# Splitting two loads of output weights into eight shares instead of sixteen, in a decode-attention kernel

## The chip, the cores and the metric

One core of a Trainium2 chip. The time is the device time of one execution, in microseconds (us); most executions of this program agree within 0.4 us. All runs used here were fast (within 1.5% of the fastest run of the same kernel). Traces come from profiled executions, which took as long as the others.

## The reference, cut to what matters

The kernel computes two decode-attention blocks, A and B, for a batch of 4 with one query token each, and puts their outputs side by side:

```python
# shortened: block B; A lets four query heads share each of its key-value heads
q = (x @ wq).reshape(B, Sq, H, Dh).transpose(0, 2, 1, 3)
scores = einsum("bhqd,bhkd->bhqk", q, k_cache) * Dh ** -0.5
o = einsum("bhqk,bhkd->bhqd", softmax(scores), v_cache)
out = o.transpose(0, 2, 1, 3).reshape(B, Sq, H * Dh) @ wo
```

B has 32 heads of 128 and reads all 8192 cached positions; A has 8 key-value heads and reads the last 2048. B's keys and values alone are 537 MB, so this is a kernel of loads.

## The kernel before

The parts that the change touches. B's work goes by pairs of heads (`hp`, 16 of them) and by batch entry; a pair's two heads of one entry are one load of keys and one of values, 4 MB each, 128 partitions of 32 KB. The output weights of a pair are 256 KB, 128 partitions of 2 KB, in a single-buffered tile `wos`:

```python
def dma_wos(hp):
    src = B_wo[2 * hp * P:2 * (hp + 1) * P, :].rearrange("(p r) n -> p (r n)", r=2)
    sch.add_dma("sp", lambda e: e.dma_start(wos[:, :, :].rearrange("p r n -> p (r n)"), src), "d_wos",
                waits=[("fin", NCA + 4 * hp - 1)] if hp else [], key=("wos", hp))
# ... (cut)
for kind, c in loads:
    if kind == "k" and c >= NCA and (c == NCA or (c - NCA) % 4 == 3 and c > NCA + 3):
        dma_wos((c - NCA) // 4)
    dma_kv(kind, c)
```

All large loads are issued from SyncE's queue in this order. The kernel counts a load as landed when its semaphore has gained 16. The trace of before shows the sixteen: each load has sixteen landing marks, and the queue has 2804 packets of 4 bytes (9 ns each), 16 for each of its 175 loads and 4 for a store of 4 rows.

## Time and profile before

| | before |
|---|---|
| time, median (lowest to highest) of 6 runs | 1374.13 us (1373.97 to 1374.33) |
| bytes read | 587.2 MB, 428 GB/s over the span |
| SyncE's queue, share of 16 DMA engines' time | 99.8% |
| TensorE busy | 86% |

The lines and their reading are in the prediction below.

### The profile page before, as it was taken

What the parts mean: (1) busy time and instruction counts of PE and PEld (TensorE: products, weight loads), DVE (VectorE), ACT (ScalarE), POOL (GpSimd) and SP (SyncE); (2) the same over time, 40 slices, a digit from 0 to 9 for tenths busy, and PEclk for the clock granted to TensorE, in tenths of its full rate; (3) what the DMA queues carried; (4) which work ended last, traced back from release to release, by engine and by line L of the source; (5) the groups of instructions that cost most, each with busy time, mean ns of one, the idle gap of its engine ahead of it and who ended that gap; (6) DMA issues with size and microseconds to landing.
All of it is one profiled execution on the core that took longest, in us unless ns stands there. A gap on an engine that the chain in (4) does not pass through costs nothing.

```text
span 1372.6 us, 59967 instructions
## 1 busy us (share of the span) xinstructions
PE 1176.5 (86%) x27065; PEld 1132.9 (83%) x27067; DVE 656.6 (48%) x1434; ACT 434.7 (32%) x650; POOL 7.3 (1%) x28
## 2 busy tenths in 40 slices
PE   4888898889888888988888888888898888888888
PEld 4777898888888888888888878888898888888888
DVE  1775454445444444454445444444454444444544
ACT  1553232333223322332233323322333233323322
POOL 2000000000000000000000000000000000000000
PEclk9998999999999999999999999999999999999999
DMA  9999999999999999999999999999999999999998
GB/s 400 423 424 432 429 433 428 433 432 432 432 431 433 429 434 428 434 430 434 430 434 430 430 433 432 432 431 433 429 433 431 434 429 434 430 432 432 432 427 352
DMA packets 25261, 587.53 MB, mean 428 GB/s; under 512 B 2820, under 2 KB 2840, under 8 KB 6296
## 3 DMA queue, kind: packets, MB, share of 16 engines
q1 hardware_dynamic: 25208, 587.22, 99.8%
q8 instruction: 16, 0.26, 0.1%
q14 instruction: 5, 0.04, 0.0%
q10 hardware_dynamic: 32, 0.01, 0.0%
HBM read 587.21 MB, written 0.01 MB: 428 GB/s over the span
## 4 chain that ended last, share of the span: by engine, by line
DMA 65%; PE 33%; issue 1%; DVE 1%; ACT 0%; SPq 0%; DVEq 0%
DMA kv<-in_B_k_cache_dram 57%; PE tr L408 21%; PE sc L410 9%; DMA kv<-in_A_k_cache_dram 5%; DMA kv<-in_B_v_cache_dram 3%; PE po L410 2%; PE fin L410 1%; PE ms L410 0%; ACT kt L476 0%; DVE sA L527 0%; SPq L365 0%; ACT pba L597 0%; PE ms L408 0%; DVE zA L683 0%; DVE rm L536 0%
## 5 line engine op out<-in xcount | busy, mean ns | idle before, releaser
L408 PE MATMUL tr<-identb,kv 128*128 128x128 bf16 x8704 | 697.9, 230 | 148.8 <-DMA kv<-in_B_k_cache_dram 141.5
L478 DVE COPY kt<-tr 128x1024 bf16<-128x1024 bf16 x736 | 502.6, 690 | 457.1 <-PE tr L408 452.7
L408 PEld LDWEIGHTS tr<-identb,kv 128*128 128x128 bf16 x8704 | 552.9, 104 | 165.2 <-DMA kv<-in_B_k_cache_dram 81.7
L476 ACT ACTIVATE kt<-tr 128x1024 bf16<-128x1024 bf16 x352 | 359.3, 1023 | 666.8 <-PE tr L408 666.7
L410 PE MATMUL sc<-qb,kt 128*128 128x64 bf16 x8704 | 446.2, 196 | 14.3 <-ACT kt L476 12.8
L410 PEld LDWEIGHTS sc<-qb,kt 128*128 128x128 bf16 x8704 | 366.4, 100 | 26.0 <-ACT kt L476 20.2
L410 PE MATMUL po<-pbb,kv 128*128 128x64 bf16 x8320 | 284.4, 192 | 4.5 <-issue 3.9
L410 PEld LDWEIGHTS po<-pbb,kv 128*128 128x128 bf16 x8320 | 263.2, 97 | 7.1 <-issue 4.1
L577 ACT ACTIVATE pbb<-sc,negb 64x128 bf16<-64x128 f32 x128 | 51.6, 403 | 254.3 <-DVE negb L564 253.5
L541 DVE TENSOR_REDUCE rm<-sc 64x1 f32<-64x128 f32 x128 | 37.0, 289 | 56.6 <-PE sc L410 55.7
L553 DVE TENSOR_REDUCE gm<-ms 1x2 f32<-1x128 f32 (+1 forms) x72 | 20.1, 279 | 48.4 <-PE ms L408 48.4
L564 DVE COPY negb<-ms 128x1 f32<-128x1 f32 (+1 forms) x72 | 11.4, 158 | 47.0 <-PE ms L410 46.8
L410 PE MATMUL ms<-identf,gx 1*128 1x1 f32 (+1 forms) x144 | 27.2, 256 | 0.8 <-DVE zA L683 0.8
L666 DVE TENSOR_TENSOR oz<-po,rz 128x8 bf16<-128x8 f32 x33 | 5.5, 166 | 40.7 <-PE po L410 40.7
L410 PEld LDWEIGHTS ms<-identf,gx 1*128 1x128 f32 (+1 forms) x144 | 21.1, 182 | 4.6 <-DVE zA L683 0.9
L577 ACT ACTIVATION_READ_ACCUMULATOR pbb<-sc,negb 64x1 f32 x128 | 23.7, 185 | 0.0
L410 PE MATMUL po<-pba,kv 128*128 128x64 bf16 x512 | 20.5, 199 | 3.5 <-issue 2.1
L410 PEld LDWEIGHTS po<-pba,kv 128*128 128x128 bf16 x512 | 17.9, 102 | 5.7 <-ACT pba L597 4.2
L408 PE MATMUL ms<-identf,rm 128*1 128x128 f32 (+1 forms) x72 | 19.5, 271 | 2.4 <-DVE rm L536 2.3
L557 DVE TENSOR_SCALAR gx<-gm 1x128 f32<-1x128 f32 (+1 forms) x72 | 16.0, 222 | 2.5
L683 DVE CAST zB<-ms 64x8 bf16<-64x8 f32 x64 | 10.5, 164 | 9.2 <-PE ms L410 8.7
L410 PE MATMUL ms<-xT,kv 128*128 128x4 bf16 x256 | 7.1, 166 | 8.8 <-DMA kv<-in_A_wq_dram 5.0
(61 smaller groups left out, 173.9 us busy)
## 6 DMA issues: line engine op xcount, KB each, us to landing
kv<-in_B_k_cache_dram SPq DMA_DIRECT2D x63, 4096.0 KB, 26.5
kv<-in_B_v_cache_dram SPq DMA_DIRECT2D x63, 4096.0 KB, 30.9
kv<-in_A_k_cache_dram SPq DMA_DIRECT2D x8, 2048.0 KB, 14.8
kv<-in_A_v_cache_dram SPq DMA_DIRECT2D x8, 2048.0 KB, 16.2
kv<-in_A_wq_dram SPq DMA_DIRECT2D x1, 4096.0 KB, 12.5
kv<-in_B_wq_dram SPq DMA_DIRECT2D x1, 4096.0 KB, 27.1
wor<-in_A_wo_dram SPq DMA_DIRECT2D x8, 512.0 KB, 9.8
wos<-in_B_wo_dram SPq DMA_DIRECT2D x16, 256.0 KB, 20.3
```

Source lines behind the costliest of these rows:

```text
L408: sch.add("pe", lambda e: e.transpose(o, l, r), waits, key)
L410: sch.add("pe", lambda e: e.matmul(o, l, r, start=start, stop=stop), waits, key)
L476: sch.add("act", lambda e: e.activation(dst, src, ACTF.Copy), waits=waits, key=("ev", s))
L478: sch.add("dve", lambda e: e.tensor_copy(dst, src), waits=waits, key=("ev", s))
L541: sch.add("dve", lambda e, src=src, pp=pp: e.tensor_reduce(out=rm[pp, m, 0:1], in_=src, axis=AX.X, op=ALU.max), waits=[("S", ch["s_last"]) ...
L553: sch.add("dve", lambda e: e.tensor_reduce(out=gm[0:C, m, 0:U], in_=src, axis=AX.X, op=ALU.max), waits=[("trm", c)], key=("gmax", c))
L557: sch.add("dve", lambda e: e.tensor_scalar(out=dst, in0=gv, scalar1=-scale, scalar2=None, op0=ALU.mult), waits=[("gmax", c)], key=("gx", c))
L564: sch.add("dve", lambda e: e.tensor_copy(negb[:, m, 0:C], ms[:, col:col + C]), waits=[("bc", c)], key=("negb", c))
L577: sch.add("act", lambda e, src=src, pp=pp, n=n, u=u: e.activation(probs_of(c)[pp, :, u], src, ACTF.Exp, bias=negb[pp, m, 0:1], scale=scale ...
L666: sch.add("dve", lambda e: e.tensor_tensor(out=o, in0=i0, in1=i1, op=ALU.mult), waits=waits, key=("oT", c))
L683: sch.add("dve", lambda e, src=src, pp=pp: e.tensor_copy(z[pp, :].rearrange("p (r b) -> p r b", r=k), src), waits=[("sm", c)] + free if h ...
```

## The change

The intent: move some bytes away from half of the DMA engines. If a load's source has an outer dimension of 8, its rows should be dealt out in eight shares to eight engines, and the other eight would be left free.

```diff
             src = B_wo[2 * hp * P:2 * (hp + 1) * P, :].rearrange("(p r) n -> p (r n)", r=2)
-            sch.add_dma("sp", lambda e: e.dma_start(wos[:, :, :].rearrange("p r n -> p (r n)"), src), "d_wos",
+            dst = wos[:, :, :].rearrange("p r n -> p (r n)")
+            if hp in (1, 2):
+                (s, _), (x, n) = src.ap
+                src = bass.AP(src.tensor, src.offset, [[16 * s, 8], [s, 16], [x, n]])
+            sch.add_dma("sp", lambda e: e.dma_start(dst, src), "d_wos",
                         waits=[("fin", NCA + 4 * hp - 1)] if hp else [], key=("wos", hp))
```

An access pattern is a list of [step, count]. `s` is the step from one row to the next, so `[16 * s, 8], [s, 16]` names the same 128 rows in the same order as `[s, 128]`.

## The prediction

> **What bounds the kernel now.** I read the page's slices first (part 2), then the queues (part 3), then the chain of waits, then the times at which each load landed.
>
> ```profile
> PE   4888898889888888988888888888898888888888
> PEclk9998999999999999999999999999999999999999
> DMA  9999999999999999999999999999999999999998
> GB/s 400 423 424 432 429 433 428 433 432 432 432 431 433 429 434 428 434 430 434 430 434 430 430 433 432 432 431 433 429 433 431 434 429 434 430 432 432 432 427 352
> ...
> q1 hardware_dynamic: 25208, 587.22, 99.8%
> q8 instruction: 16, 0.26, 0.1%
> q14 instruction: 5, 0.04, 0.0%
> ...
> DMA 65%; PE 33%; issue 1%; DVE 1%; ACT 0%; SPq 0%; DVEq 0%
> ```
>
> The DMA row is at 9 in 39 of 40 slices and the rate stays at 427 to 434 GB/s through the middle. One queue, SyncE's, fills the time of all 16 DMA engines (99.8%). TensorE is busy too, but the chain of waits is mostly DMA, and its last part is a load:
>
> ```profile
> 1329.13 0.43 SPq L365
> 1329.56 0.35 issue
> 1329.92 39.14 DMA kv<-in_B_v_cache_dram
> 1369.06 0.05 issue
> 1369.11 0.42 PE po L410 x8
> ```
>
> The last piece of values is issued at 1329.92 us and lands at 1369.06; 3.5 us of small work follow to the end at 1372.6. So the end is the moment at which the last byte lands, plus a fixed tail. Loads are never issued too late to keep the engines fed: in the table of issues a 4 MB load of keys lands 26.5 us after its issue and one of values 30.9 us, while the engines need 4194 KB / 432 GB/s = 9.7 us for one, so two to three loads are always queued ahead.
>
> ```profile
> kv<-in_B_k_cache_dram SPq DMA_DIRECT2D x63, 4096.0 KB, 26.5
> kv<-in_B_v_cache_dram SPq DMA_DIRECT2D x63, 4096.0 KB, 30.9
> ...
> wos<-in_B_wo_dram SPq DMA_DIRECT2D x16, 256.0 KB, 20.3
> ```
>
> A load counts as landed when the **last** of its 16 engines is done, so I looked at the engines one by one. The trace has no engine number, but every packet starts 4 ns before the end of the one ahead of it on its engine, and every engine gets the same sequence of sizes, so the packets can be sorted into 16 chains. At the last large load of keys (landing at about 1343 to 1347 us) the chains stand behind the earliest by (us, worked out):
>
> ```
> eight chains without a q8 packet in the body: 0.00 0.06 0.20 0.34 0.34 0.56 1.40 2.13
> eight chains with q8 packets:                 1.96 3.15 3.25 3.28 3.32 3.38 3.41 3.81
> ```
>
> The trace's sixteen landing marks of each load say the same: first to last 0.8 us at 12 us, 2.3 us at 43 us, 3.8 us at 144 us, and 3.7 us ever after. The steps fall where a q8 packet (16 KB of instructions) goes: 15 of them between 19.7 and 168.2 us, each setting its chain back by about 1.5 us, going round the same eight chains in the same order. Seven of these chains are hit twice, one once. After 168 us [...]no more come until 1368 us. The two stragglers among the other eight carry q14 packets (8 KB; at 55 and 151 us on one, at 83 and 1333 us on the other). So eight engines end late because of work that isn't the kernel's data, and the change is about shifting data to the others.
>
> [...]the 4-row loads of x and the 4-row store at 128 us left exactly 4 data packets each. The four chains of that store are 0.00, 0.20, 1.40 and 2.13 of the list above (matched by the phase of their packets)[...]. [...]q8 shows 16 packets of 16384 bytes. [...]
>
> **The change, part by part.** It removes nothing: the same 256 KB go to the same rows of the weight tile, for pairs 1 and 2 (issued at 220.1 and 298.5 us). No instruction of TensorE, VectorE or ScalarE moves, no wait is added. What changes is the split: [...]with 16 rows of 2 KB on each of engines 0 to 7 and nothing on 8 to 15.
> - One share of eight rows costs an engine 8 packets x 84 ns (median of the 2 KB packets) = 0.67 us less overlaps of 4 ns each, plus a 9 ns mark: 0.65 us. The landing marks give 0.66 us (values at 316.08, weights at 316.74, first engine). I use 0.66.
> - Each changed load puts engines 0 to 7 back by 0.66 us and brings 8 to 15 forward by 0.66 us. Two: 1.32 us each way, and it stays, as spreads stay once made.
> - If the first line is engines 0 to 7 and the second 8 to 15, the latest of the second becomes 3.81 - 1.32 = 2.49, the latest of the first 2.13 + 1.32 = 3.45. The last landing moves from 3.81 to 3.45: **0.36 us earlier**. One split load alone would give max(3.15, 2.79), 0.66 us; the second overshoots because of the one chain with two q14 packets.
> - SyncE's issue of a weight load takes 0.33 us[...]. It lies beside 20 us of queued loads and costs nothing.
>
> Sum: 1374.1 - 0.36 = 1373.7 us. Perfect balance would put all chains at their mean of 1.91, a gain of 1.9 us or 0.14%, so this lever can't reach 2% in either direction.
>
> **The rivals.**
> - *The late eight aren't 8 to 15.* [...]If the instruction queue used, say, engines 4 to 11, some of the late chains would get 1.32 us more: 3.81 + 1.32 = 5.13, the end 1.3 us later, 1375.4 us. Against it: [...]the author chose exactly eight shares. I give it 1 in 8.
> - [...]Then the late eight lose by contention what they gain by skipping, nothing improves, and the time is 1374.1 to 1374.4. [...]I give it 1 in 6.
> - *The q14 stragglers come at other places* in unprofiled executions. Without them the first line's latest would be about 0.6 + 1.3 = 1.9, the second's 2.49 rules, and the full 1.32 us is gained: 1372.8 us. 1 in 10.
> - *The transfer is hidden anyway*, TensorE being the bound. Then nothing moves: 1374.1 us. Against it, TensorE's transposes sat idle 141.5 us waiting for keys of B.
>
> **Range and chances.** Three runs before lie within 0.36 us of each other, as much as the gain that I expect, so the sign is hardly to be seen in a median. The rivals span 1372.8 to 1375.4. I take 1373.7, with 1372.8 to 1375.0 for 8 in 10, which leaves out most of the wrong-half case. Two per cent are 27 us; no case comes near, so 0.99 for within 2%.
>
> **What would show it.** In the changed kernel's profile: (1) the count of 2 KB packets stays (2 x 128), but in each of the two loads 8 landing marks come from the engines and not 16, so the table of issues may lose its landing time for the weights; (2) landings of keys after 240 us come some 0.66 us earlier than before, and after 317 us about 0.36 us earlier, no further gain; (3) the spread of a load's sixteen marks, 3.8 us at 232 us before, falls to about 3.2 after the first and is about 3.4 after the second, with the order turned over: the former first line last; (4) 32 KB packets near 240 and 318 us not stretched beyond 1.22 us, or the port rival holds; (5) a spread grown to 5 us would be the wrong half. The prediction is wrong if the end moves by over 1.3 us, for which an engine would have to starve or the copy be split otherwise than in eight.

The forecast's sum is 1374.1 - 0.36 = 1373.7 us. Its premise: each of the two loads goes out in eight shares to eight engines; take that as the author's assumption. All that the trace shows towards it is that the copies of 4 rows left 4 data packets and 4 landing marks each. The trace numbers no engines: read "0 to 7" as the eight that such a load was expected to use, "8 to 15" as the others. That "0 to 7" are the first line of the list was assumed too. The second rival, called ports from here on, had an engine write, with its neighbouring rows, partitions that others were writing at that time, and both slow down.

## The result, and the profile after

| | before | after |
|---|---|---|
| time, median of 6 runs | 1374.13 us | 1374.14 us |
| lowest to highest | 1373.97 to 1374.33 | 1374.03 to 1374.33 |

The ratio of after to before is 1.0 (95% interval 0.9987 to 1.0013): the same. Ratios here are the mean time of one kernel's fast runs over that of the other's fast runs of the same rounds, so not quite the ratio of the medians.

From the page of the kernel after, the slices and the queues (packets, MB, share of 16 engines' time), and the issues of the weights (KB, median us to landing):

```profile
DMA  9999999999999999999999999999999999999998
...
DMA packets 25261, 587.53 MB, mean 428 GB/s; under 512 B 2820, under 2 KB 2840, under 8 KB 6296
...
q1 hardware_dynamic: 25208, 587.22, 99.8%
...
wos<-in_B_wo_dram SPq DMA_DIRECT2D x16, 256.0 KB, 20.6
```

The queue has the same 25208 packets as before. That is the line that gives it away. The 4-byte packets among them are the landing marks, one for each engine that takes part in a load: 16 for each of the 175 loads, as before. A load on eight engines has eight marks fewer, so two of them should have left 25192, the count that two real splits left later (next section). And the landing time of the weights is still there, 20.6 us; on the page of those two real splits it is missing.

The chain of waits at the end (start, duration, what) ends as before's does. The last piece was issued 1.0 us earlier and took 0.9 us longer; its landing is before's to within 0.2 us:

```profile
1328.88 40.05 DMA kv<-in_B_v_cache_dram
1368.94 0.05 issue
1368.98 0.42 PE po L414 x8
```

The last byte lands at 1368.94 us; before it was 1369.06. For the engines one by one I use the trace's sixteen landing marks of a load (us behind the first), here those of the keys that follow the first changed load, worked out from the trace. Below, a chain is the sequence of packets of one DMA engine:

```
before  248.06 + 0.0 0.1 0.3 0.3 0.4 0.4 0.9 2.0 2.2 3.1 3.3 3.3 3.3 3.5 3.5 3.8
after   248.54 + 0.0 0.0 0.0 0.2 0.3 0.4 1.5 1.5 1.6 2.7 2.8 2.9 2.9 3.0 3.1 3.2
```

The spread after looks smaller, as the prediction had hoped. But the last load of keys *ahead* of the changed one has the same 3.25 us, first to last (before's has 3.85). The difference was there before the change could act; it is one execution against another.

Then I compared the two built programs, instruction by instruction. They differ in source lines and tracebacks and in nothing else. The source of the two loads, as built, in elements:

```
before                   [[1024, 128], [1, 1024]]
after                    [[1024, 128], [1, 1024]]
reordered (next section) [[1024, 8], [8192, 16], [1, 1024]]
```

The eight by sixteen, which walks on evenly, was folded into 128 again in the build; the reordered one, which doesn't, was left as it is.

### The profile page after: what moved, and what is told of

Its sections match the earlier page's. It is cut to its first block, busy times and chain, and to the rows that moved or that the text cites. A ratio compares the mean times of both kernels' runs of the same rounds, so it can differ in the third digit from the quotient of the medians.

```text
span 1372.4 us, 59967 instructions
## 1 busy us (share of the span) xinstructions
PE 1177.7 (86%) x27065; PEld 1135.4 (83%) x27067; DVE 656.5 (48%) x1434; ACT 435.3 (32%) x650; POOL 7.4 (1%) x28
## 3 DMA queue, kind: packets, MB, share of 16 engines
q1 hardware_dynamic: 25208, 587.22, 99.8%
## 4 chain that ended last, share of the span: by engine, by line
DMA 60%; PE 37%; issue 1%; DVE 1%; ACT 1%; SPq 0%; DVEq 0%
DMA kv<-in_B_k_cache_dram 55%; PE tr L412 23%; PE sc L414 9%; DMA kv<-in_B_v_cache_dram 3%; PE po L414 2%; DMA kv<-in_B_wq_dram 2%; PE fin L414 1%; PE ms L414 1%; DVE sA L531 0%; ACT kt L480 0%; DVE rm L540 0%; PE ms L412 0%; SPq L369 0%; DVE sA L529 0%; ACT pba L601 0%
## 6 DMA issues: line engine op xcount, KB each, us to landing
wos<-in_B_wo_dram SPq DMA_DIRECT2D x16, 256.0 KB, 20.6
```

## The experiments

Theory **folded**: the change never reached the chip, so nothing can be learnt from its time about shares of eight. Rival **balanced**: the shares were eight, and gains and losses cancelled. Beyond that, two models of what real shares of eight would do: **engines** (the prediction's: bytes move from late engines to early ones, and only that), and **ports** (an engine that writes partitions which another engine's load is writing costs both; the word is a label here, no trace shows a port).

All differences below are against before in the same rounds. By the 2% rule only the fourteen splits in eight shares are slower (ratio 1.0247, interval 1.0232 to 1.0263). The other differences of 2 us and more are under 2%, but the interval of none of them includes 1.

### As written, on fourteen loads

```diff
-            if hp in (1, 2):
+            if 1 <= hp <= 14:
```

> The change exactly as written, on fourteen loads (pairs 1 to 14) in place of two; results right. 'Folded': the built program is that of before, so the queue's packets stay at 25208, every load of weights has 16 marks from engines, and the time is 1374.1 within 0.4. 'Split, but balanced' (the tested change did reach the chip and two loads happen to cancel out): 14 x 8 marks fewer, 25096 packets, and with fourteen loads the shift shows, about 35 us longer as in the reordered run, 1409.

Measured: 1374.30 us (4 runs), before 1374.32 in the same rounds, ratio 1.0 (0.9985 to 1.0015). The queue's line on its page:

```profile
q1 hardware_dynamic: 25208, 587.22, 99.8%
```

Seven times the change is still nothing, down to the count of packets. "Balanced" falls: the next run shows what fourteen real splits cost.

### A split that the build can't fold: two, fourteen and one load

The rows are taken in another order, so that the outer step is not 16 inner ones. The weights of these pairs land in wrong rows: the results are wrong (relative error 0.12 to 0.44), and only the time and the trace count.

```diff
-                src = bass.AP(src.tensor, src.offset, [[16 * s, 8], [s, 16], [x, n]])
+                src = bass.AP(src.tensor, src.offset, [[s, 8], [8 * s, 16], [x, n]])
```

> The same two loads, with the source's rows in another order that can't be folded (step of one row inside the outer dimension of 8), so that the built program keeps 8 shares; the results of pairs 1 and 2 are wrong on purpose. Theory 'folded' (the tested change built to the very program of before, the model of engines is right): only now 8 landing marks of the two loads come from engines instead of 16, the late chains come forward and the early ones go back by 0.66 us a load, the spread of 3.2 to 3.8 us turns over, and the time is 0.3 to 0.8 us lower, about 1373.6. Rival 'ports': 8 marks too, but the late chains gain nothing, 1374.1 to 1374.4. Rival 'wrong half': the spread grows to about 5 us, 1375.4.

> The same for fourteen of the sixteen loads (pairs 1 to 14), to make the shift large. 'Folded' with the model of engines: the early chains go back by 14 x 0.66 = 9.2 us and the others come forward as much, so the latest becomes 2.1 + 9.2 = 11.3 in place of 3.8: 7.5 us longer, 1381.6. 'Ports': the late chains don't come forward; the early ones still go back, so also longer, but the other half's landing marks stay where they were. 'Wrong half': 3.8 + 9.2 = 13, 9.2 us longer, 1383.3.

> A reordered source with 8 shares on one load alone (pair 1; results wrong on purpose). From two loads (+5.0 us) and fourteen (+34.6 us) about 2.5 us a load: 1376.6. The first model of engines, without ports, would have had 0.66 us less, 1373.5.

| loads split | time, us | against before | per load | packets in the queue |
|---|---|---|---|---|
| 1 | 1376.64 | +2.3 | 2.3 | 25200 |
| 2 | 1379.17 | +5.0 | 2.5 | 25192 |
| 14 | 1408.81 | +34.6 | 2.5 | 25096 |

The packets fall by exactly 8 a load: now the shares are eight. From the page with two split loads, the queue, and the issues of weights, whose landing time is gone since not every load has 16 marks:

```profile
q1 hardware_dynamic: 25192, 587.22, 99.7%
...
wos<-in_B_wo_dram SPq DMA_DIRECT2D x16, 256.0 KB
```

and the end of its chain of waits, where the last landing is 5 us later and the tail of small work is the same:

```profile
1335.10 39.00 DMA kv<-in_B_v_cache_dram
1374.10 0.05 issue
1374.15 0.43 PE po L414 x8
```

The first two expectations of time missed under every theory named: the model of engines had 1373.6 and 1381.6, the highest rival 1375.4 and 1383.3. The third, taken from the first two results, held. So shares of eight lose 2.3 to 2.5 us a load here, where the model of engines gained 0.3 to 0.7. The GB/s of the slices between 175 and 1320 us of the run with two show where: dips to 403 and 404, at the two loads alone.

```profile
GB/s 434 429 403 432 429 404 433 430 429 434 430 432 433 430 432 431 432 432 430 432 433 432 429 434 430 432 430 431 435 430 429 433 430 432 433 430 434 431 430 433
```

The engines are not idle there. In the stretch from 236 to 256 us, first in the kernel after, then with two real splits, the queue fills all of the engines' time (in before, 99.8% of the queue's packets between 200 and 900 us start 3 to 5 ns before the end of another, so the share can pass 100%) and moves less:

```profile
q1 hardware_dynamic: 431, 8.62, 100.6%
...
q1 hardware_dynamic: 398, 7.80, 101.1%
```

The packets themselves take longer. Between 200 and 900 us of the run with fourteen, 967 of 1152 packets of 2 KB are stretched by over 10% (median 122 ns in place of 84), and 533 of 8915 packets of 32 KB, which belong to the loads of keys and values at the same moment, some of them to nearly 2 us in place of 1.22. Before, 7 and 1 are stretched.

### The control: reordered, but sixteen shares

```diff
+            if 1 <= hp <= 14:
+                (s, _), (x, n) = src.ap
+                src = bass.AP(src.tensor, src.offset, [[s, 16], [16 * s, 8], [x, n]])
```

> Control: the same fourteen loads with a reordered source whose outer dimension is 16, so 16 shares remain and only the order of rows and the form of the instruction change (results wrong on purpose). All theories of shares: 16 marks a load, 1374.1 us within 0.4. If the reordering or the longer instruction itself costs time, the time grows here as it does with 8 shares.

Measured: 1397.01 us, +22.8, or 1.6 a load, with 25208 packets and 16 marks:

```profile
q1 hardware_dynamic: 25208, 587.22, 99.8%
...
wos<-in_B_wo_dram SPq DMA_DIRECT2D x16, 256.0 KB, 22.3
```

The expectation of "all theories of shares" missed. So most of the cost is not the number of shares. What is left is the reordering: the far rows in memory, the longer form of the instruction, or which engine now writes which partition.

### Right results, natural row order: one load in sixteen pieces of 8 rows

```diff
+            if hp == 1:
+                for i in range(16):
+                    p = slice(8 * i, 8 * i + 8)
+                    sch.add_dma("sp", lambda e, p=p: e.dma_start(dst[p, :], src[p, :]), "d_wos",
+                                waits=waits if i == 0 else [], key=("wos", hp) if i == 15 else None)
+                return
```

> Right results: one load (pair 1) as sixteen loads of 8 rows, each of which can go to 8 engines only. 'Folded' with the model: 16 x 8 marks; early chains back by 0.7 us, late ones forward by 0.66 us; latest max(2.1 + 0.7, 3.8 - 0.66) = 3.15 in place of 3.8, so 0.5 to 0.7 us less: 1373.5. If sixteen issues on SyncE (16 x 0.33 = 5.3 us) drain the queue of loads, the time grows by up to 5 us.

Measured: 1376.83 us, +2.6, with right results. The time expected under the model of engines, 1373.5, missed. The queue has 25320 packets, so each of the sixteen left 8 marks. The sixteen issues took 5.4 us of SyncE and drained nothing: the DMA row of its page stays at 9 in all slices but the last. Rows, order and form are natural, and the cost is that of a reordered load all the same. Here, too, packets are stretched by over 10% between 200 and 900 us: 104 of 2 KB and 63 of 32 KB.

### Own ports, other ports, far rows

The deciding group. Eight extra loads of 8 rows each, at pairs 1 to 8, go into a scratch tile that nothing reads. The results stay right. The targets were chosen by an assumption on which engine writes which partitions in an ordinary load; no trace gives an engine's partitions, so "own" and "other" are names for two sets of partitions. The three kernels have the same number and size of packets and differ in one place each:

```diff
+            if 1 <= hp <= 8:
+                for i in range(8):
+                    to, rows = <below>
+                    sch.add_dma("sp", lambda e, to=to, rows=rows: e.dma_start(wox[to, :], src[rows, :]), "d_wox")
  own ports:    to = 32 * (i // 4) + i % 4, step 4, eight of them        rows = 8 * i to 8 * i + 7
  other ports:  to = the same + 64                                       rows the same
  far rows:     to = as own ports                                        rows = i, i + 16, ... (32 KB apart)
# ... (cut: the scratch tile, its semaphore and the wait for it at the end)
```

> The kernel of before plus, at pairs 1 to 8, eight extra loads of 8 rows of 2 KB each into a scratch tile that nothing reads (results stay right). Target partitions step by 4 within 0 to 63[...]. 'Ports' (what costs in the shares of eight is that an engine writes partitions that another engine's load is writing at that time): no packet is stretched, 2 KB packets stay at 84 ns and 32 KB ones at 1.22 us; the early eight chains go back by 8 x 8 x about 88 ns = 5.6 us, the late eight not at all; latest about 2.1 + 5.6 = 7.7 in place of 3.8: about 3.9 us longer, 1378. 'Small pieces' (8 rows a load are dear in themselves): packets stretched as in the run with one load in sixteen pieces, time above 1382.

> The same extra loads, same rows and same steps, but 64 partitions higher[...]. 'Ports': 2 KB packets stretched to 100 to 130 ns and some 32 KB packets far above 1.22 us, about 12 us of engine time lost per pair (half of the 23 to 28 us seen with 128 rows), both halves of the engines pushed back, so 3 to 7 us longer than the run on own ports: 1381 to 1385. 'Small pieces' or 'source rows': the same time as on own ports.

> As on own ports, but the eight rows of each extra load lie 32 KB apart in memory, as the rows of the reordered load with 16 shares did. 'Ports': the same as own ports within 0.4 us, no stretched packets. 'Source rows' (the reordered loads were dear because of far rows in memory): 2 KB packets stretched and several us longer.

| | time, us | against before | 2 KB packets stretched over 10% | 32 KB packets |
|---|---|---|---|---|
| own ports | 1381.49 | +7.2 | 3 of 1664 | 34 of 9103 |
| other ports | 1393.14 | +18.9 | 689 of 1664 | 434 of 8930 |
| own ports, far rows | 1381.43 | +7.2 | 5 of 1664 | 33 of 9096 |

(Packets between 200 and 900 us; before has 7 of 1152 and 1 of 9142.) The GB/s of the slices from 228 to 880 us, first for own ports, then for other ports:

```profile
GB/s 428 430 434 432 430 428 430 433 434 428 426 432 434 428 430 434 424 436 430 426 435 432 426 438 423 429 432 434 430 426 434 432 426 440 426 426 434 428 432 432
```

```profile
GB/s 388 440 426 434 432 390 432 433 428 436 384 428 438 430 430 384 428 434 428 436 378 436 426 436 426 384 430 438 424 437 377 434 430 432 427 386 434 426 432 433
```

The second has eight dips to between 377 and 390, one for each of the eight pairs. The first has none. The same rows, sizes and steps, 64 partitions higher, cost 11.7 us more over eight pairs. Far rows in memory cost nothing (1381.43 us against 1381.49). So "source rows" and "small pieces" fall, and of the theories named only **ports** is left. What the runs show of it is that the partitions written make the difference; that they are written by two engines at once is the author's reading. On other ports a load's first landing mark goes back too, not the last alone, as expected: at the end of that run it is 12.3 us later than before's and its last 19.2 us, on own ports 0.7 and 7.5 (from the marks). The size was missed: 1393.14 lies above the 1381 to 1385 expected. What the engines share there, if anything, the traces don't show.

The size for own ports missed too (+7.2 in place of +3.9), and the traces say why for the most part. In the run with far rows the packets could be sorted into sixteen chains without one left over, and the extra packets mark eight of them. Before the first extra load the chains stood, in us behind the earliest (worked out; * had instruction packets of q8):

```
eight with extra packets: 0.00 0.08 0.18 0.21 0.81 2.34 3.28* 3.55*
the other eight:          0.29 0.31 1.86* 3.31* 3.34* 3.38* 3.47* 3.92*
```

Two of the late chains are among the eight with extra packets. By the landing marks each pair put the last landing back by 0.7 to 1.0 us, in most pairs more than the 0.70 us of eight packets with their marks, and the latest grows from 3.55 and not from 2.34. Own ports were not quite free, either: 34 packets of 32 KB were stretched (median 1.46 us), about four a pair, where none were expected. That stays open.

### Do instruction blocks delay loads?

The lateness of the late chains was put down to instruction packets. To test that, 2048 one-element memsets were added on GpSimd:

```diff
# ... (cut: the tile wox)
+        for i in range(2048):
+            sch.add("pool", lambda e, i=i: e.memset(wox[0:1, i:i + 1], 0.0), waits=["c_sel"])
```

> The kernel of before with 2048 one-element memsets on GpSimd behind its set-up (results right)[...]. If such a block sets back a chain by 1.5 us and goes round the same eight chains[...], the spread grows from 3.2 to 3.8 us to about 5 and the time by about 1.5 us, to 1375.6. If the blocks go to the other eight chains, the spread shrinks to some 2 to 3 us and the time stays at 1374 within 0.5 (nothing is gained at the late end). If instruction blocks don't delay loads, nothing changes.

Measured: 1383.15 us (1381.51 to 1385.92), +8.9, results right. From its page:

```profile
q8 instruction: 16, 0.26, 0.1%
q14 instruction: 21, 0.17, 0.0%
```

A "block" is a packet like q8's of 16 KB. None of the outcomes written down came. q8 is unchanged. q14 has 16 packets of 8 KB more, which is 64 B for each memset, and in the landing marks a single engine falls behind, up to 9.7 us at 93 us of the span. So instruction packets do set loads back, but the 16 that came with GpSimd's memsets went by q14 and burdened one engine, while q8's 15 in the body went round eight. After about 200 us the spread is only 1.3 us, and the time is lost all the same. The marks, load against load of before, show how: the last landing is 9.2 us later at 83 us and 8.3 at the end; the first is on time up to 59 us, 5 us late from 87 us and 10.9 us late from 189 us. Between 56 and 195 us the queue fills 96.5% of the engines' time (before: 100.3%). So the other engines fell idle until they stood beside the late one. That they waited for buffers which it kept is an inference, and so is the rest of the way to 8.9 us.

## Why the prediction was right or wrong

The time lay in the range, at 1374.14 against 1373.7, and within 2%. That was luck: the change never reached the chip, and a kernel that stays the same stays in any range around its own time. The mechanism was wrong, and no rival named what happened.

- **What bounds the kernel** held: full DMA engines (99.8%), the last landing and then a fixed tail (3.5 us before, after and with two real splits). In all the runs whose marks are given, the end moved with the last landing: of the profiled executions the span grew by 5.0 us with two real splits, 36.4 with fourteen, 7.4 on own ports, 19.1 on other ports and 8.3 with the memsets, the last landing by 5.0, 36, 7.5, 19.2 and 8.3.
- **The step that failed**: "What changes is the split", to eight shares. It was assumed from the pattern as written, and the instruction carries 128. The runs show 25208 packets where 25192 were needed, and the same with fourteen loads. The prediction's first sign, eight marks in place of sixteen, was the right one to look at: it failed at once. What I read of the change was its source; the pattern as built could have been read before predicting. The prediction's last sentence has "the copy be split otherwise than in eight" only as a way to a longer time. Here it was split otherwise, in sixteen as before, and the time showed nothing.
- **The size of a share**, 0.66 us, was not put to the test by this change. Extra shares of the same size on own ports cost 0.7 to 1.0 us a pair. The gain of 0.36 us worked out from it wouldn't have come from a real split either, for the next two reasons.
- **"If the first line is engines 0 to 7 and the second 8 to 15"** was wrong, and the rival of the wrong half (1 in 8) was right in part. Two late chains are among the eight that the extra loads of 8 rows went to. By the list above, two real splits to the same eight without any other cost would put the latest at 3.55 + 1.32 = 4.87 in place of 3.92 us, some 1 us later (an estimate from those figures).
- **Ports** (1 in 6) is the rival that the runs on own and other ports left standing, and it had the size wrong: "nothing improves, and the time is 1374.1 to 1374.4". A real split costs 2.3 to 2.5 us a load. From the stretched packets of the run with fourteen: about 277 us of engine time more than before over the nine loads in the window, / 9 / 16 = 1.9 us an engine, plus the 0.66 us of the share, 2.6 in all; measured 2.5. (An estimate: it spreads the loss evenly over the engines.) I had let contention only take back what a skipped share gives. In the run with fourteen a load's first landing mark is in the end 26 us later than before's and its last 36 us: neither half comes forward, and the time is lost, not moved.
- **A hidden transfer** falls: fourteen real splits moved the end by 34.6 us. **The stragglers of q14** at other places were not tested. One reading was loose: the spread is 3.8 us from 144 to about 450 us and 3.7 only after that. The prediction that the lever can't reach 2% held for what it was about, evening out: its bound of 1.9 us. For losses it was no bound, as fourteen real splits cost 2.5%.

No version here beats both kernels. Sharing out to eight engines lost wherever it really happened (2.3 to 2.6 us a load), and the two kernels compared are one program.

## What to carry to other kernels

Read the access pattern as built, or count packets and landing marks, before reasoning about what a rewritten pattern does: here a split that walks on evenly was folded away (25208 packets in place of 25192). Before dealing out a small load otherwise, or to other partitions, measure what it does to the large loads around it: here 256 KB dealt out otherwise cost 1.6 to 2.6 us, with packets of 32 KB stretched from 1.22 to nearly 2 us, and the same 64 small loads cost 7.2 or 18.9 us by the partitions that they wrote. When a change that should shift something measures as exactly nothing, multiply it before believing in a balance.
